# A guest place for one weight granule, the router's scores behind phase one, and a tail with other layouts and queues

## The chip, the core and the metric

The kernel runs on one core of a Trainium2 chip. TensorE (PE) multiplies matrices, VectorE (DVE) and ScalarE (ACT) work on whole tiles and copy results out of PSUM, GpSimd (POOL) and SyncE (SP) mostly issue transfers here. Transfers issued by SP, ACT and POOL are carried out by the same 16 DMA engines. The metric is the device time of one execution in microseconds (us); lower is better. Times of the trace are counted from the start of the span.

## What is computed

One layer norm of x (2048 rows of 1024) feeds two branches; their results are added to x. The first is attention over 64 segments of 32 rows with a memory of 8 rows that goes from segment to segment; the second sends the two best-scored rows through a gated feed-forward block. Cut to what matters:

```python
xn = _layernorm(x)
mem = mem0
for s in range(64):                       # 32 rows each, 32 heads of 128
    h = concatenate([mem, xn[:, 32*s:32*s + 32]], axis=1)
    q, k, v = h @ Wq, h @ Wk, h @ Wv      # by head
    p = softmax(where(mask, q @ k.T * scale, -1e9))
    o = (p @ v) @ Wo
    mem = o[:, :8]
    outs.append(o[:, 8:])
r = xn @ w_r
idx = argsort(-r)[:, :2]                  # the two routed rows
y = (silu(xn[idx] @ w_gate) * (xn[idx] @ w_up)) @ w_down
y = y * sigmoid(r[idx])
return x + concatenate(outs) + (xn + scatter(y, idx))
```

All tensors are bf16. Wq, Wk, Wv and Wo hold 8 MB each.

## The kernel before

**Granules.** The four attention weights are cut into 64 granules of 128 x 2048 (512 KB). Granules 0 to 47 belong to six phases (`PHASES`): p = 0 is the first half of Wq (granules 0 to 7), p = 1 the first half of Wk (8 to 15), p = 2 and 3 their second halves, p = 4 and 5 the halves of Wv; granules 48 to 63 are Wo. 44 are resident in SBUF; each has a home, a place of its own (`home`, `room`, `load_resident`). 17 are streamed: every segment takes them anew from a copy in DRAM (`wsc`) through five slots (`fetch`, pool `wstream`). Granule 15, the last of phase one (p = 1), is one of them. Three more (0, 7, 27) are kept partly in PSUM. The homes of Wv granules are `v_homes`: the first eight are one area, `big0`, the others stand alone; `v_homes[8]` is the home of granule 43 and `hx = v_homes[-1]` that of granule 46.

**Main rows and left rows.** Of each segment 24 rows and the 8 rows of memory are the main rows; they make the 32 columns of `ST`, and segment after segment they go through the phases (L745), attention and Wo (`project`, L798). The last 8 rows of every segment, 512 rows in all, are the left rows. Their Q and K (`left_qk`, L500) and V (`left_v`, L527) are worked out for all segments while segment 0 has the weights at hand, behind the main rows' matmuls of each phase; they go to DRAM (`ql_d`, `vl_d`), and each segment takes its own part back. What attention gives for left rows is stored after each segment in DRAM (`ol_d`, `store_sums`, L604). The tail, behind the last segment, loads all of that as `OTA` (`load_left_out`, L595, 16 loads of 256 KB: eight by POOL during the last segment, eight by SP), multiplies it by Wo (`left_rows_out`, L874, two halves of two blocks), adds x and stores four blocks (L881).

**Segment 0.** Phase zero's granules lie in homes and in four of the slots, granule 11 in the fifth. When phase p is done, `left_done(p)` fetches as many granules as slots have come free. All of the following is in program order, so each engine meets it in that order. DVE takes the row statistics of x (`row_stats`, L238) during phase zero. In phase one PE does the 32 main matmuls (L745), `left_qk` for head 0, then for heads 1 and 2; then come `spread` (four small matmuls on PE, L250, and copies on DVE, L255 to L257), which lays out means and deviations, the 16 steps of `router_tile` on DVE (a `tensor_scalar`, L263, and a multiply-and-sum, L265, on 128 x 1024 each), and `left_qk` for heads 3 to 15. `sd_rows` (L242 on DVE, a square root on ACT, L243) stands ahead of that. At the end of phase one's `left_qk` DVE copies `QKL` (L513); in the next phase ACT copies from it to `KT` (L640) and DVE copies the transposed keys there (L642), and then PE may do the scores (L650). Later the router's scores go to DRAM and come back as one row (`router_out`, `router_top`), of which DVE finds the two highest. The x tiles that statistics and router read lie in the area `big1`, over which the second half's left Q and K (`GA`) are written from phase two on.

**Feed-forward.** In the tail SP loads w_gate, w_up and w_down (`fetch_moe`, L438 and L441) into homes that have come free; `gate_up` (L903) and the down matmuls (L930) follow. POOL takes the two routed rows back out of the output (L916), DVE adds (L933), and SP stores both (L936), each behind a load of its row number into a register.

Of the kernel before, what the change touches and what calls it, by code (L numbers as in the profile page):

```python
# [21 lines left out]
HALF_KEPT = 27  # L22
KEPT_HERE = (FIRST_KEPT, NEXT_KEPT, HALF_KEPT)
NEG = -30000.0

# [4 lines left out]
def kernel(  # L30
# [86 lines left out]
    vl_d = [dram.tile([16, 16, XL, 2, P], BF16, name=f"vl_d{t}") for t in range(4)]  # L117
    ol_d = [dram.tile([16, P, XL * H], BF16, name=f"ol_d{t}") for t in range(4)]

# [88 lines left out]
    def xt(t):  # L208
        return XP[:, t // 2, (t % 2) * D:(t % 2 + 1) * D]
# [50 lines left out]

    def router_tile(t):
        XR = home(hx, [P, D], BF16, "XR")
        nc.vector.tensor_scalar(out=XR[:, :], in0=xt(t), scalar1=RI16[:, t, 0:1], scalar2=RI16[:, t, 1:2],  # L263
                                op0=ALU.subtract, op1=ALU.mult)
        nc.vector.tensor_tensor_reduce(out=XR[:, :], in0=XR[:, :], in1=WRB, scale=1.0, scalar=0.0,  # L265
                                       op0=ALU.mult, op1=ALU.add, accum_out=RF[:, t:t + 1])

# [153 lines left out]
    to_copy = list(streamed)  # L421
    flow += [(s, g) for s in range(NSEG) for g in (streamed if s else first_streamed)]

# [54 lines left out]
    for g in range(KC, 32):  # L478
        if g in first_streamed:
            if len(queued) < N_SLOT:  # L480
                fetch()
        else:
            load_resident(g)
        if g >= 8 and g < 15:
            load_x(g - 7)
    for g in v_homes[8:-1]:
        load_resident(g)
# [5 lines left out]
    def left_qk(mat, half, Gs, between, h0=0, h1=16):  # L493
        if mat == 0 and h0 == 0:
            gathered[half] = area(f"big{half}", [P, NSEG, 256], "GA")
        GA = gathered[half].rearrange("p s (m i q r) -> p s m i q r", m=2, i=4, q=4)
        for h in range(h0, h1):
            PSG = psA.tile([P, 512], F32, tag="acc", name="PSG")
            for kc in range(KC):
                nc.tensor.matmul(PSG[:, :], lhsT=part(Gs[kc], h // 4)[:, P * (h % 4):P * (h % 4 + 1)], rhs=XLT[:, :, kc, :],  # L500
                                 start=(kc == 0), stop=(kc == KC - 1))
            nc.scalar.copy(out=GA[:, :, mat, h % 4, h // 4, :], in_=PSG.rearrange("p (s r) -> p s r", r=XL))  # L502
            if h % 2 == 1 or mat + half == 0:
                next(between, None)
        if h1 < 16:
            return
        for _ in between:
            pass
        if mat == 1:
            G3 = gathered[half]  # L510
            if half == 0:
                qkl[0] = one.tile([P, 2, 2, 4, 4, XL], BF16, tag="bA", name="QKL")
            nc.vector.tensor_copy(out=qkl[0][:, half].rearrange("p m i q r -> p (m i q r)"), in_=G3[:, 0, :])  # L513
            if half == 0:
                for k in range(NSEG // 8):
                    store_left(half, k)
# [31 lines left out]
    def left_done(p):  # L548
        for g in range(8 * p, 8 * (p + 1)):
            if g in first_streamed:  # L550
                fetch()
        if p == 1:
            area("big0", [P, 8, 2048], "W8A")
# [40 lines left out]
    def load_left_out(k, queue):  # L594
        queue.dma_start(out=areas["big0"][:, 4 * k:4 * k + 4, :], in_=ol_d[k // 4][4 * (k % 4):4 * (k % 4) + 4].rearrange("s p c -> p s c"))  # L595

# [5 lines left out]
    def store_sums():  # L602
        s, t = unsaved.pop(0)
        nc.gpsimd.dma_start(out=ol_d[s // 16][s % 16], in_=t.rearrange("p r h -> p (r h)"))  # L604

# [15 lines left out]
    for s in range(NSEG):  # L621
# [7 lines left out]
        def transposes(mat, half, XB):  # L629
# [8 lines left out]
            else:  # L638
                KT[half] = one.tile([P, 16, NK], BF16, tag="kt", name="KT")
                nc.scalar.copy(out=KT[half].rearrange("p (i q) k -> p i q k", i=4)[:, :, :, 32:NK],  # L640
                               in_=qkl[0][:, half, 1, :, :, :])
                nc.vector.tensor_copy(out=KT[half][:, :, 0:32], in_=pv)  # L642

# [94 lines left out]
        for p, (mat, half) in enumerate(PHASES):  # L738
# [13 lines left out]
            if mat < 2:  # L752
# [4 lines left out]
                if s == 0:  # L757
# [4 lines left out]
                    if p == 1:  # L762
                        nc.gpsimd.tensor_copy(out=GATE, in_=gathered[0][:, 0, 128:132])
                        copy_blocks(6)
                        sd_rows(MV[:, 1:NT, :], VE[:, 1:NT])
                        left_qk(mat, half, Gs, kept, 1, 3)
                        h1 = 3
                        spread(1, NT)
                        for t in range(NT):
                            router_tile(t)  # L770
                    elif p == 2:
# [96 lines left out]
    def left_rows_out(k):  # L868
        WD = [[psK.tile([P, 512], F32, name=f"WD{2 * b + c}", tag=f"kept{2 * b + c}") for c in range(2)] for b in range(2)]
        for b in range(2):  # L870
# [7 lines left out]
            for c in range(2):  # L878
                xc = x[:, 512 * c:512 * (c + 1)]
                nc.vector.tensor_tensor(out=xc, in0=xc, in1=WD[b][c][:, :], op=ALU.add)  # L880
            nc.scalar.dma_start(out=out2.rearrange("(t s r) d -> t s r d", t=4, s=16)[2 * k + b, :, XM:SEG, :], in_=x)  # L881

# [51 lines left out]
    for c in range(2):  # L934
        v = nc.sync.value_load(I8[0:1, c:c + 1], min_val=0, max_val=S - 1)
        nc.sync.dma_start(out=routed_out(v), in_=quarters(c))  # L936

# [34 lines left out]
```

## Time and profile before

| | |
|---|---|
| median of 3 runs | 1859.54 us (1859.37 to 1860.27) |
| the profiled execution | 1847.92 us, span 1846.3 us |
| PE busy | 1555.7 us (84%) |
| DVE, ACT, POOL busy | 880.4 us, 774.9 us, 320.9 us |
| moved by DMA | 678.50 MB, mean 367 GB/s |
| segment 0 | from the start to about 242 us |
| last segment's end, tail | from about 1760 us |

All views are of the one profiled execution, which is shorter than the runs; only differences are carried over. A row of a timeline gives start and duration in us, the engine, the line of the kernel, the operation with the tiles it writes and reads, the number of merged instructions, and in brackets the idle time ahead of it with what ended that. A row of the waits gives who waited for whom, the sum in us, how often, and the longest. A row of the stretches gives start, end and length, the busy time of PE, weight loads, DVE, ACT and POOL, the granted TensorE clock (1.00 is full), the DMA engines' share and GB/s. A row that lists one line's instructions gives their least, median and greatest duration in ns and the first and last start. DMA-issuing rows of SP and ACT are marked SPq and ACTq.

### The profile page before, as it was taken

What the parts mean: (1) busy time and instruction counts of PE and PEld (TensorE: products, weight loads), DVE (VectorE), ACT (ScalarE), POOL (GpSimd) and SP (SyncE); (2) the same over time, 40 slices, a digit from 0 to 9 for tenths busy, and PEclk for the clock granted to TensorE, in tenths of its full rate; (3) what the DMA queues carried; (4) which work ended last, traced back from release to release, by engine and by line L of the source; (5) the groups of instructions that cost most, each with busy time, mean ns of one, the idle gap of its engine ahead of it and who ended that gap; (6) DMA issues with size and microseconds to landing.
All of it is one profiled execution on the core that took longest, in us unless ns stands there. A gap on an engine that the chain in (4) does not pass through costs nothing. (4 is left out here: it accounts for less than half of the span.)

```text
span 1846.3 us, 70379 instructions
## 1 busy us (share of the span) xinstructions
PE 1555.7 (84%) x30358; PEld 828.2 (45%) x30370; DVE 880.4 (48%) x2711; ACT 774.9 (42%) x2019; POOL 320.9 (17%) x592
## 2 busy tenths in 40 slices
PE   6889978888888888888888888888888888888888
PEld 3334434444444444444444444444444444444465
DVE  6631235555554454555555555444455555555420
ACT  2333134444444444444444444444444444444400
POOL 1020111111111111111111111111111111111200
PEclk9999989999999999999999999999999999999988
DMA  9684899999999999999999999999999999999996
GB/s 361 218 301 135 261 367 391 393 394 394 368 387 376 368 389 383 392 386 372 396 393 396 396 394 394 385 386 389 386 391 394 397 382 393 395 395 395 392 364 251
DMA packets 223288, 678.50 MB, mean 367 GB/s; under 512 B 46848, under 2 KB 54320, under 8 KB 222976
## 3 DMA queue, kind: packets, MB, share of 16 engines
q1 hardware_dynamic: 196768, 623.79, 88.3%
q0 software_dynamic: 24192, 46.54, 7.5%
q8 instruction: 237, 3.88, 0.8%
q10 hardware_dynamic: 2016, 3.67, 0.6%
q14 instruction: 75, 0.61, 0.1%
HBM read 652.90 MB, written 29.89 MB: 370 GB/s over the span
## 5 line engine op out<-in xcount | busy, mean ns | idle before, releaser
L745 PE MATMUL PSm<-wres,ST 128*32 128x512 bf16 x6400 | 500.7, 382 | 0.0
L745 PEld LDWEIGHTS <-ST 128*32 128x32 bf16 x12288 | 313.3, 96 | 349.5 <-issue 107.4
L745 PE MATMUL PSm<-g,ST 128*32 128x512 bf16 x3084 | 307.3, 384 | 46.6 <-DMA g<-wsc 38.2
L411 ACT COPY BK<-KEPT 128x512 bf16<-128x512 bf16 x315 | 189.3, 601 | 175.0 <-PE WO L798 65.1
L798 PEld LDWEIGHTS <-OT 128*32 128x32 bf16 x8192 | 209.2, 97 | 85.6 <-issue 69.3
L754 ACT CAST XB<-PSm 128x512 bf16<-128x512 f32 x256 | 150.2, 587 | 132.7 <-PE PSm L745 131.1
L642 DVE COPY KT<-BT 128x512 bf16<-128x512 bf16 x128 | 51.8, 405 | 290.6 <-PE BT L632 290.6
L798 PE MATMUL WO<-W8B,OT 128*32 128x256 bf16 x4096 | 186.2, 276 | 0.0
L745 PE MATMUL PSm<-W8A,ST 128*32 128x512 bf16 x2048 | 182.7, 380 | 0.0
L587 POOL DMA_DIRECT2D QKL<-ql_d x63 | 46.5, 738 | 755.7 <-ACT OTL L714 740.6
L798 PE MATMUL WO<-g,OT 128*32 128x256 bf16 x2560 | 130.7, 277 | 53.1 <-DMA g<-wsc 48.8
L832 POOL DMA_DIRECT2D out_dram<-XN x256 | 130.7, 526 | 173.9 <-DVE XN L828 173.8
L779 ACT CAST VM<-PSm 128x512 bf16<-128x512 f32 x128 | 80.3, 627 | 114.0 <-PE PSm L745 114.0
L411 DVE COPY BK<-KEPT 128x512 bf16<-128x512 bf16 x189 | 80.2, 425 | 72.3 <-ACT BK L411 36.9
L632 PEld LDWEIGHTS <-XB 128*128 128x128 bf16 x1024 | 57.9, 98 | 106.6 <-ACT XB L754 101.5
L674 DVE TENSOR_REDUCE DN<-BS 128x8 f32<-128x320 f32 x128 | 62.9, 491 | 88.0 <-ACT BS L669 88.0
L632 PE MATMUL BT<-IDENT,XB 128*128 128x128 bf16 x1024 | 101.7, 222 | 3.1
L500 PE MATMUL PSG<-XLT,wres 128*128 128x512 bf16 x352 | 101.3, 390 | 0.8 <-ACT GA L502 0.7
L637 ACT COPY QT<-BT 128x512 bf16<-128x512 bf16 x128 | 74.9, 585 | 53.4 <-PE BT L632 51.4
L659 DVE TENSOR_TENSOR BS<-BS,CT 128x96 f32<-128x96 f32 (+1 forms) x256 | 59.7, 233 | 76.5 <-PE BS L652 72.0
L745 PE MATMUL PSm<-BK,ST 128*32 128x512 bf16 x567 | 76.7, 388 | 22.2 <-DVE ST L369 22.2
L828 DVE CAST XN<-WO 128x256 bf16<-128x256 f32 x64 | 27.2, 424 | 127.5 <-PE WO L798 127.5
(171 smaller groups left out, 2278.9 us busy)
## 6 DMA issues: line engine op xcount, KB each, us to landing
g<-wsc SPq DMA_DIRECT2D x1071, 512.0 KB, 6.3
ql_d<-GA POOLq DMA_DIRECT2D x16, 512.0 KB, 6.3
QKL<-ql_d POOLq DMA_DIRECT2D x63, 128.0 KB, 6.2
MW<-in_B_w_gate_dram SPq DMA_DIRECT2D x16, 448.0 KB, 8.0
MW<-in_B_w_down_dram SPq DMA_DIRECT2D x14, 512.0 KB, 8.3
wres<-in_A_Wk_dram SPq DMA_DIRECT2D x12, 512.0 KB, 10.5
MW<-in_B_w_up_dram SPq DMA_DIRECT2D x12, 448.0 KB, 8.5
XP<-in_A_x_dram SPq DMA_DIRECT2D x8, 512.0 KB, 10.1
```

Of the source, the lines that this page charges most:

```text
L411: copy(out=back[g][c], in_=KEPT_COLS[g][c])
L500: nc.tensor.matmul(PSG[:, :], lhsT=part(Gs[kc], h // 4)[:, P * (h % 4):P * (h % 4 + 1)], rhs=XLT[:, :, kc, :], start=(kc == 0), stop=(kc = ...
L632: nc.tensor.transpose(out=PTq[:, il, :, :].rearrange("p j r -> p (j r)"), in_=XB[:, il * P:(il + 1) * P], identity=IDENT[:, :])
L637: nc.scalar.copy(out=QT[half][:, :, :], in_=pv)
L642: nc.vector.tensor_copy(out=KT[half][:, :, 0:32], in_=pv)
L659: nc.vector.tensor_tensor(out=S4, in0=S4, in1=m, op=ALU.add)
L674: nc.vector.tensor_reduce(out=DN[:, :], in_=S8, axis=AX.X, op=ALU.add)
L745: nc.tensor.matmul(PSm[32 * jq:32 * jq + 32, :], lhsT=ST[:, kc, :], rhs=part(Gv, jq), start=(kc == 0), stop=(kc == KC - 1), tile_position= ...
L754: nc.scalar.copy(out=XB[:, :], in_=PSm[:, :])
L779: nc.scalar.copy(out=VM[half][:, :], in_=PSm[:, :])
L798: nc.tensor.matmul(PS[32 * g:32 * g + 32, 0:256], lhsT=lhs(h), rhs=Gv[:, D * hs + 256 * g:D * hs + 256 * (g + 1)], start=False, stop=(last ...
L832: nc.gpsimd.dma_start(out=out2[s * SEG:s * SEG + XM, 256 * g:256 * (g + 1)], in_=OB[32 * g:32 * g + XM, :])
```

## The change

Granule 15 is no longer fetched through a slot in segment 0. It is loaded, early and in its turn behind granule 14, into the home of granule 43 (`v_homes[8]`), as a guest; granule 43 is loaded there when phase one is done, ahead of the `big0` loads on SP. The fetches of segment 0 after that come one place earlier.

`sd_rows`, `spread` and the router's 16 steps move from the middle of phase one to the end of phase zero (`left_done(0)`); the steps now alternate between two buffers. The copy of `QKL` (both halves) and segment 0's copies of transposed keys go from DVE to ACT.

In the tail `ol_d` is laid out by partition, so that a load takes 2 KB in one piece for each partition where it took four pieces of 512 bytes; a store writes its 128 pieces of 512 bytes at a distance of 8 KB. The four stores of left rows go from ACT to POOL. The two routed rows are stored by SP and ACT, one each, with row numbers loaded ahead of the activation.

```diff
-    ol_d = [dram.tile([16, P, XL * H], BF16, name=f"ol_d{t}") for t in range(4)]
+    ol_d = [dram.tile([P, 16, XL * H], BF16, name=f"ol_d{t}") for t in range(4)]
...
-    def router_tile(t):
-        XR = home(hx, [P, D], BF16, "XR")
...
+    def router_tiles():
+        XR = home(hx, [P, 2, D], BF16, "XR")
+        for t in range(NT):
+            nc.vector.tensor_scalar(
+                out=XR[:, t % 2, :], in0=xt(t), scalar1=RI16[:, t, 0:1], scalar2=RI16[:, t, 1:2],
+                op0=ALU.subtract, op1=ALU.mult)
+            nc.vector.tensor_tensor_reduce(out=XR[:, t % 2, :], in0=XR[:, t % 2, :], in1=WRB, scale=1.0, scalar=0.0,
+                                           op0=ALU.mult, op1=ALU.add, accum_out=RF[:, t:t + 1])
...
-    flow += [(s, g) for s in range(NSEG) for g in (streamed if s else first_streamed)]
+    flow += [(s, g) for s in range(NSEG) for g in (streamed if s else first_streamed) if s or g != GUEST]
...
     for g in range(KC, 32):
-        if g in first_streamed:
+        if g == GUEST:
+            t = res_tiles[g] = room(v_homes[8], "guest")
+            nc.sync.dma_start(out=t, in_=granule_dram(g))
+        elif g in first_streamed:
...
-    for g in v_homes[8:-1]:
+    for g in v_homes[9:-1]:
         load_resident(g)
...
-            nc.vector.tensor_copy(out=qkl[0][:, half].rearrange("p m i q r -> p (m i q r)"), in_=G3[:, 0, :])
+            nc.scalar.copy(out=qkl[0][:, half].rearrange("p m i q r -> p (m i q r)"), in_=G3[:, 0, :])
...
     def left_done(p):
         for g in range(8 * p, 8 * (p + 1)):
-            if g in first_streamed:
+            if g in first_streamed and g != GUEST:
                 fetch()
-        if p == 1:
+        if p == 0:
+            sd_rows(MV[:, 1:NT, :], VE[:, 1:NT])
+            spread(1, NT)
+            router_tiles()
+        elif p == 1:
+            res_tiles.pop(GUEST)
+            load_resident(v_homes[8])
             area("big0", [P, 8, 2048], "W8A")
...
-        queue.dma_start(out=areas["big0"][:, 4 * k:4 * k + 4, :], in_=ol_d[k // 4][4 * (k % 4):4 * (k % 4) + 4].rearrange("s p c -> p s c"))
+        queue.dma_start(out=areas["big0"][:, 4 * k:4 * k + 4, :], in_=ol_d[k // 4][:, 4 * (k % 4):4 * (k % 4) + 4, :])
...
-        nc.gpsimd.dma_start(out=ol_d[s // 16][s % 16], in_=t.rearrange("p r h -> p (r h)"))
+        nc.gpsimd.dma_start(out=ol_d[s // 16][:, s % 16, :], in_=t.rearrange("p r h -> p (r h)"))
...
-                nc.vector.tensor_copy(out=KT[half][:, :, 0:32], in_=pv)
+                (nc.vector.tensor_copy if s else nc.scalar.copy)(out=KT[half][:, :, 0:32], in_=pv)
...
                     if p == 1:
                         nc.gpsimd.tensor_copy(out=GATE, in_=gathered[0][:, 0, 128:132])
                         copy_blocks(6)
-                        sd_rows(MV[:, 1:NT, :], VE[:, 1:NT])
-                        left_qk(mat, half, Gs, kept, 1, 3)
-                        h1 = 3
-                        spread(1, NT)
-                        for t in range(NT):
-                            router_tile(t)
...
-            nc.scalar.dma_start(out=out2.rearrange("(t s r) d -> t s r d", t=4, s=16)[2 * k + b, :, XM:SEG, :], in_=x)
+            nc.gpsimd.dma_start(out=out2.rearrange("(t s r) d -> t s r d", t=4, s=16)[2 * k + b, :, XM:SEG, :], in_=x)
...
+    ends = (nc.sync, nc.scalar)
...
+    end_rows = [ends[c].value_load(I8[0:1, c:c + 1], min_val=0, max_val=S - 1) for c in range(2)]
     SG = T2[:, 64:64 + 4 * FC].bitcast(F32)
...
     for c in range(2):
-        v = nc.sync.value_load(I8[0:1, c:c + 1], min_val=0, max_val=S - 1)
-        nc.sync.dma_start(out=routed_out(v), in_=quarters(c))
+        ends[c].dma_start(out=routed_out(end_rows[c]), in_=quarters(c))
```

More of the change, by code (lines that the diff above doesn't have):

```diff
@@ L23 @@
 KEPT_HERE = (FIRST_KEPT, NEXT_KEPT, HALF_KEPT)
+GUEST = 15
 NEG = -30000.0
@@ L259 @@
     hx = v_homes[-1]
-    def router_tile(t):
-        XR = home(hx, [P, D], BF16, "XR")
[L263 to L266, printed above, removed]
+    def router_tiles():
[6 more added lines that the diff above has]
+                                           op0=ALU.mult, op1=ALU.add, accum_out=RF[:, t:t + 1])
     def router_out():
```

## The prediction, made before the changed kernel was run

> **What bounds the kernel now.** I read the page first, then PE's waits in two stretches, then timelines around the long waits. The page's slices:
>
> ```profile
> span 1846.3 us, 70379 instructions
> ...
> PE   6889978888888888888888888888888888888888
> ...
> PEclk9999989999999999999999999999999999999988
> DMA  9684899999999999999999999999999999999996
> ```
>
> A slice is 46 us. From the sixth on DMA is full and PE is not; the first five, which hold segment 0, are the only place inside the kernel where DMA has room. PE's waits from 250 us to 1740 us, then those up to 250 us:
>
> ```profile
> PE WO L798 <- DMA g<-wsc: 44.8, 86, 1.8
> PE PSm L745 <- DMA g<-wsc: 38.2, 88, 1.5
> ```
>
> ```profile
> PE BS L650 <- ACT KT L640: 6.7, 1, 6.7
> PE PSm L745 <- DMA g<-in_A_Wk_dram: 5.5, 1, 5.5
> PE WO L798 <- DMA g<-in_A_Wo_dram: 3.1, 2, 2.8
> PE PSV L527 <- ACT VM L779: 2.2, 1, 2.2
> ```
>
> In the middle PE waits for streamed granules, and the stream restarts each transfer when PE frees a slot. So segments 1 to 63 are a chain that takes its length from bytes moved and its start from the end of segment 0. The change leaves the chain alone and acts before and behind it. In segment 0 two single waits stand out, 6.7 and 5.5 us; the change is aimed at both.
>
> **The guest.** Granule 15 is asked for only when phase zero frees a slot, at 51.98, and PE stands before it:
>
> ```profile
> 29.34 0.38 SPq L205 DMA_DIRECT2D XP<-in_A_x_dram  x1
> 30.62 7.19 SPq L136 DMA_DIRECT2D wres<-in_A_Wq_dram  x6
> ...
> 51.98 0.33 SPq L386 DMA_DIRECT2D g<-in_A_Wk_dram  x1
> ```
>
> ```profile
> 53.06 0.83 PE L745 MATMUL PSm<-wres,ST 128*32 128x512 bf16 x12
> ...
> 60.73 0.62 PE L745 MATMUL PSm<-g,ST 128*32 128x512 bf16 x4 [5.54 <-DMA g<-in_A_Wk_dram]
> ```
>
> ```profile
> 60.70:64.70 4.00, 3.97 (x13) 1.32 (x13) 0.00 (x0) 0.58 (x1) 0.00 (x0) 0.50 0.48 189
> ```
>
> ```profile
> wres<-in_A_Wk_dram SPq DMA_DIRECT2D x12, 512.0 KB, 10.5
> ```
>
> The last x tile is issued at 29.34, so the guest goes out between it and 30.62 and lands some 10.5 us later, near 41, twelve before its use. Term A: -5.5. After the wait the granted clock is 0.50 for 4.0 us of dense matmuls, which take twice their time: term B, -2.0 (0 to -2.3). Bytes do not change: granule 43 is loaded later by as much as the guest is early, so what SP issues between (phases two and three) is one transfer later, about 1.3 us by SP's pace there (7.19 for six), with 30 us of cover. Granule 43's load stands on SP behind one fetch and ahead of the eight `big0` loads, which then are about 1.3 us later; both are for phases four and five, and this stretch shows the room:
>
> ```profile
> 126.00:175.00 49.00, 45.15 (x307) 20.47 (x307) 14.61 (x35) 21.18 (x35) 4.38 (x7) 1.00 0.37 120
> ```
>
> **The router.** DVE before:
>
> ```profile
> 53.44 0.18 DVE L242 TENSOR_SCALAR MISC<-MISC 128x15 bf16<-128x15 bf16 x1
> 68.78 0.87 DVE L255 COPY BS<-BT 96x30 f32<-96x30 f32 x4 [15.16 <-PE BT L250]
> ...
> 69.80 0.45 DVE L263 TENSOR_SCALAR XR<-XP,MISC 128x1024 bf16<-128x1024 bf16 x1
> ...
> 99.27 0.22 DVE L513 COPY QKL<-GA 128x256 bf16<-128x256 bf16 x1
> ```
>
> ```profile
> 53.16 0.59 ACT L502 CAST GA<-PSG 128x512 bf16<-128x512 f32 x1 [1.36 <-PE PSG L500]
> ...
> 91.16 0.58 ACT L502 CAST GA<-PSG 128x512 bf16<-128x512 f32 x1 [1.14 <-PE PSG L500]
> 99.58 0.30 ACT L640 COPY KT<-QKL 128x128 bf16<-128x128 bf16 x1 [7.83 <-DVE QKL L513]
> ```
>
> ```profile
> 91.06 1.05 PE L745 MATMUL PSm<-wres,ST 128*32 128x512 bf16 x16
> ...
> 92.81 0.39 PE L745 MATMUL PSm<-wres,ST 128*32 128x512 bf16 x4
> 99.93 0.23 PE L650 MATMUL BS<-KT,QT 128*32 128x40 bf16 x4 [6.73 <-ACT KT L640]
> ```
>
> ```profile
> 99.90:103.00 3.10, 3.07 (x42) 1.24 (x43) 1.89 (x6) 0.58 (x1) 1.17 (x3) 0.53 1.02 407
> ```
>
> The router holds DVE from 69.80 to 99.27, 29.5 us or 1.84 a tile; `QKL` is queued behind it, `KT` behind that, PE behind `KT`. DVE had lain idle for 15.16 us before. Now `spread` comes at the end of phase zero, and PE meets it at 53.06: statistics end at 53.62, the square root follows ACT's eviction of 53.75 and takes about 0.2 (an estimate, from the 0.18 of DVE's step on the same 15 columns), so the four small matmuls run near 54.0 to 54.2. Queued behind them on PE is all of phase one. Term C, the added wait: +1.0 (0.6 to 1.5).
>
> Phase one then ends 5.5 + 2.0 - 1.0 = 6.5 earlier, at 84.5 for 91.0. The router starts as long after `spread`'s first copy as before (69.80 - 68.78 = 1.0), so near 55.4 for a copy near 54.4, and ends at 84.9. Nothing in phase one needs DVE. Two buffers change little, since both steps run on the one engine; I cost them at nothing (0 to -1.6 for sixteen times 0.1, off the path). PE reaches the scores at 86.7. On ACT the last eviction ends at 85.2, then the `QKL` copy (0.4, between 0.30 for 128 columns and 0.59 for 512), `KT` from it (0.3) behind PE's transposes, and the transposed keys (0.6), now on ACT too: 86.9 with the hand-over. A wait of about 0.3 stays of 6.7: term D, -6.4 (-5.9 to -6.7). The low clock after it (0.53 for 3.1 us) goes as well: term E, -1.5 (0 to -1.6).
>
> Half one pays for ACT's extra copies without any gain, as DVE was free there: scores about 0.4 later, and the chain over DVE, exponent and L779 on which PE waits 2.2 is later by that. Term F: +0.4 (0 to +0.6).
>
> POOL's first six granule copies are issued behind head 0's eviction, so about 7 us earlier and beside the router, and must write while early loads end. Before, POOL issued eight stores beside it:
>
> ```profile
> 92.04 4.47 POOL L519 DMA_DIRECT2D ql_d<-GA  x8 [22.86 <-ACT GA L502]
> ```
>
> That is 0.56 each, no different from its 0.57 elsewhere (below), and the copies are first read in segment 1: nothing. Everything later in segment 0 (W8B, Wo, the stream) is issued behind PE's progress, so it moves along. Segment 0: -5.5 - 2.0 + 1.0 - 6.4 - 1.5 + 0.4 = -14.0.
>
> The Trainium skill (TensorE: Matmul & The Clock Gate, Part 1) says that an idle window of about 3.4 us halves the clock and a busy one restores it. The trace agrees after both waits (0.50, 0.53); by it the new wait of 1 us costs no clock, and if it did, C would be about +3.
>
> **The tail.** Loads of left sums, and rates without and with them:
>
> ```profile
> L595 POOL DMA_DIRECT2D OTA<-ol_d x8: 747/749/781, 1746.8 to 1752.0; - x8
> ```
>
> ```profile
> 1755.75 0.62 PE L798 MATMUL WO<-g,OT 128*32 128x256 bf16 x8 [2.19 <-DMA g<-wsc]
> ...
> 1759.21 0.62 PE L798 MATMUL WO<-g,OT 128*32 128x256 bf16 x8 [1.13 <-DMA g<-wsc]
> ```
>
> ```profile
> 1780.00:1787.00 7.00, 6.95 (x33) 4.63 (x33) 0.00 (x0) 0.00 (x0) 0.00 (x0) 1.00 1.03 408
> 1790.00:1795.00 5.00, 5.00 (x194) 4.97 (x193) 1.28 (x2) 0.00 (x0) 0.00 (x0) 0.74 1.17 317
> ```
>
> Full DMA moves 408 GB/s with weights alone and 317 while SP's left sums go along. Eight loads are 2.1 MB: 6.6 us at 317, 5.1 at 408. Those that POOL issues run beside the last two granules PE waits for, 2.19 and 1.13. At most 1.5 us come free there, but the loads may also take a larger share of each turn. I take half, term G: -0.7 (-1.6 to +1.0). SP's eight gain as much, but PE is then at gate and up and later waits for no load: nothing.
>
> The four stores go to POOL. Only the last matters, since POOL fetches the routed rows behind it and DVE adds into them:
>
> ```profile
> 1835.79 1.21 POOL L916 DMA_DIRECT2D T<-out_dram  x2 [73.17 <-DMA out_dram<-XLS]
> ```
>
> ```profile
> T<-out_dram POOLq DMA_DIRECT2D x2, 2.0 KB, 2.5
> ```
>
> ```profile
> 1840.74 0.48 DVE L933 SCALAR_TENSOR_TENSOR T<-YP,SIG,T 128x256 bf16<-128x256 f32 x1 [5.91 <-PE YP L930]
> ```
>
> ```profile
> L604 POOL DMA_DIRECT2D ol_d<-OTL x64: 556/573/580, 247.9 to 1753.8; - x64
> ```
>
> The two fetches are issued by 1837.0; DVE starts at 1840.74, released by PE. At 2.5 us from issue to landing about 1.2 us are free. A store from POOL costs 0.57 to issue: nothing, +1 if it lands 2 us later. SP's two final stores:
>
> ```profile
> L936 SPq DMA_DIRECT2D out_dram<-T x2: 602/650/698, 1841.2 to 1843.3; - x2
> ```
>
> The second starts 2.1 us behind the first, with a register load between; on ACT it starts with the first. Term H: -2.0 (-1.5 to -2.1). Nothing hides it, as the span ends on that store.
>
> The strided stores of `ol_d` are the unknown in the chain: no row shows 512-byte pieces written 8 KB apart. 64 KB a segment are 0.16 us at 408 and 0.21 at 317 GB/s: +0.05 x 64 = +3.2 at the upper end, nothing at the lower, since pieces were 512 bytes before. I take nothing.
>
> **Sum.** -14.0 - 0.7 - 2.0 = -16.7. The profiled execution, 1847.92, would become 1831.2. It lies 11.6 below the median, far outside the spread of the runs (0.9), so the profile slightly changes the pace; I carry the difference over: 1859.54 - 16.7 = 1842.8.
>
> **Rivals.** *The gain is taken back at the end of segment 0.* PE waits there 3.1 us for Wo granules through slots. If DMA were the bound from the start, these waits would grow by most of the 14. For it: DMA is full from there on. Against: DMA share is 0.37 from 126 to 175, and those transfers are issued only when PE frees room. Half taken back: 1859.5 - 7 - 2.7 = 1850.
>
> *The strided stores slow the chain* (the other side). They decide from 16.7 / 64 = 0.26 us a segment, over the 0.21 that such a store takes at all at the worse rate. At double that rate's time for the store and its neighbours held up as long again, 0.4 a segment, it is +26 - 16.7: 1869. Against: they move 64 KB in a segment of about 24 us.
>
> *DVE stays the bound.* The x tiles lie under the second half's `GA`, whose first eviction falls near 88.5 now (two microseconds past the scores). The router ends at 84.9; from 2.07 us a tile on, PE would wait again, at 0.2 us a tile more by 3. It ran at 1.84 beside the same evictions. At 2.4 a tile: +5, so 1848.
>
> *The left sums' loads cost no more in small pieces.* Then 317 GB/s has another cause, such as the store beside it, G is 0 and the time 1843.5. The Trainium skill (DMA: Bandwidth & Descriptors, Specifications) speaks for this: it gives 512 bytes as the least transfer for line rate. The trace disagrees so far as those two stretches go, 317 against 408.
>
> **How the numbers follow.** The forecast (1842.8, its own range 1838 to 1847 by the bounds of C to H) has 0.66, small pieces at no cost 0.10, taken back 0.10, DVE still the bound 0.04, slower by the stores 0.07, the change showing no effect (guest and moved router not on the path after all) 0.03. The range from 1838 to 1851 leaves out the slower case and some of the rest. Within 0.2% (3.7 us), about what a measurement can tell from no change, lies 0.03; faster 0.90; slower 0.07.
>
> **What would show it.** Right: PE's wait for `g<-in_A_Wk` gone, a wait near 1 us at L250, the one at L650 under 1 us, the router between 55 and 85, granted clock 1.00 from 60 to 105, segment 1 starting near 228 for 242; the last two stores starting together. Wrong: longer waits of L798 before 235, a longer segment in the middle, evictions of phase two behind the router, POOL's fetch of routed rows ending later than PE's last matmul.

## The result and the profile after

The changed kernel takes 1840.17 us (median of 5 runs, 1829.70 to 1844.92) against 1859.37 for the kernel before (median of 5 runs in the same comparison): a ratio of 0.990, 95% interval 0.987 to 0.993. Two later comparisons gave 0.990 (0.987 to 0.993) and 0.990 (0.986 to 0.994). The forecast was 1842.8 in a range of 1838 to 1851. The profiled execution took 1829.70, with a span of 1828.1 for 1846.3 before.

The page of the changed kernel, the same slices as before:

```profile
span 1828.1 us, 70401 instructions
...
PE   6999888888888888888888888888888888888888
...
PEclk9999899999999999999999999999999999999988
DMA  9785999999999999999999999999999999999996
```

PE's second and third slices rise from 8 to 9: they hold phase one and the start of phase two. From the seventh on all three rows are as before. PE's waits up to 250 us, changed kernel:

```profile
...
PE WO L804 <- DMA g<-in_A_Wo_dram: 4.0, 2, 3.7
PE PSV L533 <- ACT VM L785: 2.2, 1, 2.2
...
PE BT L251 <- ACT MISC L244: 0.8, 1, 0.8
```

The waits of 6.7 us for `KT` and 5.5 us for `g<-in_A_Wk_dram` are gone from the list, and the new one at `spread`, 0.8, is there. One stretch shows what became of them, from the first matmuls of phase one to the scores. First the kernel before, then the changed one (columns as in the prediction: start, end and length, busy time of PE, weight loads, DVE, ACT and POOL, clock, DMA share, GB/s):

```profile
53.00:100.00 47.00, 34.73 (x210) 14.95 (x213) 30.39 (x59) 11.54 (x21) 8.76 (x17) 0.88 0.63 217
```

```profile
53.00:85.50 32.50, 32.28 (x204) 14.35 (x203) 28.02 (x54) 11.72 (x21) 4.69 (x10) 1.00 0.68 235
```

The stretch is 14.5 shorter. PE stood still in it for 47.00 - 34.73 = 12.3 us and now for 0.2: the waits. Its busy time fell by 2.4, of which 0.2 is `spread`, whose four matmuls lie just ahead of the second stretch; the clock rose from 0.88 to 1.00, so the rest is the half clock behind the first wait.

Since single terms are smaller than the scatter of the runs, every profiled execution is cut here in three: from the start to the first cast of segment 0's output (`XN<-WO` on DVE), from there to the same cast 62 segments later, and the rest with segment 63 and the tail. The column "phase one" gives when PE is done with phase zero and comes to phase one.

| kernel | median us, ratio (95%) | phase one | segment 0 ends | 62 segments | rest |
|---|---|---|---|---|---|
| before | 1859.37 | 53.1 | 241.0 | 1490.7 | 114.6 |
| changed | 1840.17, 0.990 (0.987 to 0.993) | 52.1 | 225.5 | 1489.9 | 112.7 |
| changed, again | 1839.49, 0.990 (0.987 to 0.993) | 52.8 | 226.8 | 1500.7 | 118.7 |
| changed, third | 1837.76, 0.990 (0.986 to 0.994) | 52.5 | 227.3 | 1494.4 | 114.7 |
| guest alone | 1848.26, 0.996 (0.994 to 0.999) | 53.7 | 236.2 | 1502.1 | 113.1 |
| router alone | 1846.88, 0.993 (0.991 to 0.996) | 53.8 | 234.7 | 1490.6 | 115.4 |
| guest and router | 1843.90, 0.993 (0.990 to 0.996) | 51.6 | 226.9 | 1488.7 | 114.6 |
| tail alone | 1855.68, 0.999 (0.996 to 1.002) | 51.0 | 243.1 | 1511.1 | 114.3 |
| both ends on SP | 1838.96, one run | 53.3 | 226.8 | 1497.7 | 112.7 |
| copies on DVE | 1843.50, one run | 51.9 | 226.7 | 1500.6 | 114.5 |
| router step twice | 1854.99, one run | 52.3 | 242.1 | 1496.8 | 114.5 |
| one routed row | 1836.62, one run | 51.7 | 225.3 | 1495.2 | 114.5 |
| everything small | 1840.41, 0.992 (0.989 to 0.995) | 54.1 | 229.1 | 1496.7 | 110.3 |
| table early | 1835.05, 0.988 (0.984 to 0.993) | 53.9 | 227.8 | 1493.3 | 110.9 |

Each ratio is to runs of the kernel before beside it, with medians of 1859.37 for the first pair of rows, 1858.70 for the four kernels that split the change, 1857.57 for *changed, again* and *everything small*, 1856.00 for *changed, third* and *table early*; the one-run kernels stand beside one of before of 1859.39. The first column of numbers is of runs, the others of one profiled execution each. Segment 0 is 13.7 to 15.5 shorter in the changed kernel. Phase one is reached at 51.0 and 53.1 by the two kernels with the front of before and at 51.6 to 53.9 by those with the whole front as changed: up to 2.9 us of a difference between two rows can lie ahead of all that the change touches. The rest shows no change beyond its scatter, and the middle differs by 22 us between executions, which the last section looks at.

### The profile page after: what moved, and what is told of

It is laid out like the page before. It is cut to its first block, busy times and chain, and to the rows that moved or that the text cites. A ratio compares the mean times of both kernels' runs of the same rounds, so it can differ in the third digit from the quotient of the medians.

```text
span 1828.1 us, 70401 instructions
## 1 busy us (share of the span) xinstructions
PE 1552.2 (85%) x30370; PEld 827.1 (45%) x30370; DVE 878.1 (48%) x2707; ACT 776.9 (42%) x2023; POOL 321.0 (18%) x596
## 5 line engine op out<-in xcount | busy, mean ns | idle before, releaser
L785 ACT CAST VM<-PSm 128x512 bf16<-128x512 f32 x128 | 80.1, 625 | 114.3 <-PE PSm L757 114.3
L686 DVE TENSOR_REDUCE DN<-BS 128x8 f32<-128x320 f32 x128 | 62.9, 492 | 85.4 <-ACT BS L681 85.4
## 6 DMA issues: line engine op xcount, KB each, us to landing
MW<-in_B_w_down_dram SPq DMA_DIRECT2D x14, 512.0 KB, 10.9
```

What stands on the lines that cost most here:

```text
L686: nc.vector.tensor_reduce(out=DN[:, :], in_=S8, axis=AX.X, op=ALU.add)
L785: nc.scalar.copy(out=VM[half][:, :], in_=PSm[:, :])
```

## The experiments

**The front's two halves apart, and the tail alone.** Four kernels split the change. *Guest alone* keeps `spread` and the router in phase one:

```diff
-        if g in first_streamed:
+        if g == GUEST:
+            t = res_tiles[g] = room(v_homes[8], "guest")
+            nc.sync.dma_start(out=t, in_=granule_dram(g))
+        elif g in first_streamed:
...
+            res_tiles.pop(GUEST)
+            load_resident(v_homes[8])
```

> The kernel before with the guest granule alone. Theory (each of the two waits is a loss of its own and the chain of segments carries a gain unchanged): PE's 5.5 us before granule 15 and the 2.0 us of half clock go, so segment 0's last cast (240.99 before) ends about 7.5 us earlier, near 233.5; the router still stands in the middle of phase one, starts 7.5 us earlier too, and PE's wait at the scores (6.7) stays, 6 to 7 us. Time about 7.5 us below before. Rival (the router alone sets the end of segment 0's early part, PE waits at the scores whatever comes before): the wait at the scores grows to 14 us and segment 0 ends as before. Second rival (the gain is taken back by transfers at the end of segment 0): PE's waits for Wo there grow from 5 to 12 us.

Two waits and a stretch of that kernel:

```profile
PE BS L656 <- ACT KT L646: 6.7, 1, 6.7
PE WO L804 <- DMA g<-in_A_Wo_dram: 4.0, 2, 2.9
```

```profile
60.70:64.70 4.00, 4.00 (x24) 1.86 (x22) 2.95 (x10) 1.17 (x2) 1.54 (x4) 1.00 1.02 410
92.70:97.00 4.30, 4.27 (x45) 1.65 (x46) 1.79 (x6) 0.58 (x1) 1.72 (x4) 0.50 1.03 402
```

No wait for granule 15 is left, and where the clock was 0.50 before it is full. The wait at the scores stands untouched at 6.7, followed by a half clock that lasts at least 4.3 us; so these two causes are apart. The scores come 7.2 earlier, at 92.73 (terms A and B together: 7.5), and 7.9 earlier if counted from phase one, which PE reached 0.7 later. But segment 0 ends only 4.8 earlier, for the 7.5 expected. From the first half's scores to the second's it takes 0.9 longer, under the half clock, and between the first output matmul and the cast 1.2 longer, with 0.9 of it in the wait for Wo granules, 4.0 for 3.1. This may be the rival "taken back at the end of segment 0", at a small size; *tail alone*, which has the front of before, is 0.6 longer there too.

*Router alone* leaves granule 15 in its slot:

```diff
+        if p == 0:
+            sd_rows(MV[:, 1:NT, :], VE[:, 1:NT])
+            spread(1, NT)
+            router_tiles()
...
-                        spread(1, NT)
-                        for t in range(NT):
-                            router_tile(t)
```

> The kernel before with the router behind phase zero and the copies on ACT, without the guest. Theory: the wait at the scores falls from 6.7 us to under 1, the half clock after it goes (1.5), half one pays up to 0.4; the wait of about 1 us for the spread is hidden, since PE then waits less for granule 15, which still lands near 60.7 (4.5 us for 5.5). Segment 0 ends near 233.5 (7.5 us earlier). Rival (the spread's wait comes on top and the router beside the evictions is slowed): less than 6 us gained, router over 1.9 us a tile.

Its wait and the row at the scores:

```profile
PE PSm L751 <- DMA g<-in_A_Wk_dram: 4.1, 1, 4.1
```

```profile
94.00 0.21 PE L656 MATMUL BS<-KT,QT 128*32 128x40 bf16 x4 [0.17 <-ACT KT L648]
```

The wait at the scores falls from 6.73 to 0.17 with the guest left out, and segment 0 ends 6.3 earlier, for the 7.5 expected. The wait for the granule, 5.5 before, is 4.1 here behind 0.8 at `spread`: PE waits a little sooner for something else and no longer in all.

*Guest and router* is all of the front, with the tail as before:

> Guest, router and copies on ACT, with the tail of before. Theory (segment 0 is nearly all of the gain): segment 0 ends 14 to 15.5 us earlier as in the changed kernel, and the time is within 2 us plus noise of the changed kernel, 14 to 18 us below before. Rival (the tail's edits or the strided stores give or take several us in the chain): the time differs from the changed kernel by 5 us or more.

Segment 0 ends at 226.9, 14.1 earlier: the front's gain is the changed kernel's. It is 3.0 more than 4.8 and 6.3 together, but 2.1 of that is phase one, reached at 51.6 here and at 53.7 by the guest alone; that the two halves help each other is not shown.

*Tail alone*:

```diff
-    ol_d = [dram.tile([16, P, XL * H], BF16, name=f"ol_d{t}") for t in range(4)]
+    ol_d = [dram.tile([P, 16, XL * H], BF16, name=f"ol_d{t}") for t in range(4)]
...
-            nc.scalar.dma_start(
+            nc.gpsimd.dma_start(
...
-        v = nc.sync.value_load(I8[0:1, c:c + 1], min_val=0, max_val=S - 1)
-        nc.sync.dma_start(out=routed_out(v), in_=quarters(c))
+        ends[c].dma_start(out=routed_out(end_rows[c]), in_=quarters(c))
```

> The kernel before with the tail's edits alone (layout of the left sums, stores on POOL, final stores on SP and ACT). By the prediction's terms: PE's waits for the last two granules fall by 0.7, the last store starts 2 us earlier, 2.7 us in all. By the trace of the changed kernel (ACT's final store waits until SP's has landed; waits for the last granules 4.9 for 4.0): the last store starts no more than 0.3 us earlier relative to DVE's last add, the whole within 1 us of before apart from the chain's own spread. If strided stores cost something, segments 1 to 63 take longer by 0.05 us each or 3 us in all.

0.999 (0.996 to 1.002): nothing that can be measured. Its rest is 114.3 for 114.6. It also gives a second look at the front of before: PE comes to phase one at 51.0 and waits 7.9 for granule 15, where it was 5.5. The matmul that waits for it starts at 61.04 here, at 60.73 before and at 61.07 with the router alone, whenever PE got there. So term A is worth more the sooner PE is done with phase zero.

**What holds the last store.** The changed kernel's rows for the final line, and for the tile that is stored, the time from issue to landing (of four transfers, the two fetches of routed rows and the two stores):

```profile
L943 ACTq EVENT_SEMAPHORE  x5: 38/38/5841, 1815.0 to 1825.1; - x5
...
L943 SPq DMA_DIRECT2D out_dram<-T x1: 692/692/692, 1823.3 to 1823.3; - x1
...
L943 ACTq DMA_DIRECT2D out_dram<-T x1: 1143/1143/1143, 1825.2 to 1825.2; - x1
```

```profile
DMA to landing us min/median/max: 1.8/2.7/3.5
```

ACT has its row number at hand. Its longest semaphore wait, 5.8 us, is for POOL's fetch of the routed rows and is over at 1820.9, well before DVE's last add; a later one ends at 1824.98, released by SP's store, which was issued at 1823.26 and so had landed 1.7 later. Then ACT issues. The two stores do not start together; they are 1.9 apart where they were 2.0. *Both ends on SP* takes the other queue away and keeps the early row numbers:

```diff
-    ends = (nc.sync, nc.scalar)
+    ends = (nc.sync, nc.sync)
```

> The changed kernel with both final stores on SP, row numbers loaded early as there. From DVE's last add to the span's end it took 5.5 us before and 5.3 in the changed kernel. Theory (the second store is held until the first has landed, because both write the output at a row not known beforehand): the second store starts 1.7 to 2.0 us behind the first though no register load stands between, and the end comes 5.2 to 5.5 us after the add. Rival (the prediction's: the register load between the stores made the 2.1 us): the second starts 0.7 us behind the first and the end comes 1.3 us sooner, about 4.1 us after the add.

```profile
L943 SPq DMA_DIRECT2D out_dram<-T x2: 561/629/697, 1832.7 to 1834.5; - x2
```

1.7 apart (1832.75 and 1834.48) on one queue too, although no issue takes over 0.7: neither the register load nor the queue makes the gap, and it equals the landing of a store. The end comes 5.0 behind the add, a little sooner than the 5.2 to 5.5 expected. In the kernel before, the register load lay over that wait: it ran from 1841.99 to 1843.02, and the first store had landed near 1842.96 (an estimate, 1841.25 + 1.71 as in the other kernels). *One routed row* leaves out the store of the second routed row, so that row of the output stays without its feed-forward:

```diff
-    for c in range(2):
+    for c in range(1):
         ends[c].dma_start(out=routed_out(end_rows[c]), in_=quarters(c))
```

> The changed kernel without the second of the two final stores (one routed row is not stored, so the output lacks its feed-forward part). It shows what a second store that costs nothing would give: by the theory that the second waits for the first's landing (1.7 us) and then takes its own time, the end comes about 3.3 to 3.6 us after DVE's last add for 5.3, 1.7 to 2.0 us less. Rival (the end is set by something else behind the stores): 5 us or more as now.

From the start of DVE's last add to the end of the span it takes 4.3, against 5.5 before, 5.3 changed and 5.0 with both on SP: more than the 3.3 to 3.6 expected. The landing of the last store tells more than the end of the span. It comes 4.2 after the start of that add before, 4.2 in the changed kernel, 3.9 with both on SP, and 2.2 with one store. So the change gained nothing at the landing, and its 0.2 lie in what the span still holds behind it. With one store the span ends 2.1 behind the landing, for 1.1 in the changed kernel, and the row that fills this time is POOL's last long instruction of the program:

```profile
L974 POOLq DRAIN  x3: 46/115/7970, 1826.2 to 1834.7; - x3
```

It begins with POOL's second fetch of a routed row, lasts 8.0 us here and in the changed kernel, and ends at 1834.16, 3.5 after the add's start at 1830.67; the closing steps of all engines follow at once. In the changed kernel it ends before the last store has landed. What it waits for is not shown. So the end has two bounds, and a second store that cost nothing would gain 1.2 against the kernel before, not 2.0, because the other bound is met. The two later kernels that also have both stores on SP end 5.8 and 6.0 behind the add for the same reason: their last store has landed at 3.9 too, and the drain ends at 5.0 and 5.2.

The Trainium skill (DMA: Bandwidth & Descriptors, Issuing engines are not separate DMA queues) says that several issuing engines save only the time of issuing. These runs agree: with two queues the last store lands 0.3 later than with one, as ACT takes 1.14 to issue it and SP 0.56.

**Whether the copies had to leave DVE.** *Copies on DVE* undoes only that:

```diff
-            nc.scalar.copy(out=qkl[0][:, half]...
+            nc.vector.tensor_copy(out=qkl[0][:, half]...
...
-                (nc.vector.tensor_copy if s else nc.scalar.copy)(out=KT[half][:, :, 0:32], in_=pv)
+                nc.vector.tensor_copy(out=KT[half][:, :, 0:32], in_=pv)
```

> The changed kernel with the copies of QKL and of segment 0's transposed keys back on DVE, as before the change. Theory (the router's new place alone removes the wait at the scores, since it ends about 1.5 us before phase one's last eviction): PE's wait at the scores of half zero stays under 0.5 us, both halves' scores come 0.1 to 0.4 us earlier, segment 0 ends within 0.5 us of the changed kernel (213.6 us after PE's first transpose). Rival (the copies had to leave DVE for the wait to go): the wait at the scores is 2 us or more.

DVE and PE of that kernel:

```profile
83.72 0.23 DVE L519 COPY QKL<-GA 128x256 bf16<-128x256 bf16 x1 [2.01 <-ACT GA L508]
84.41 0.43 DVE L654 COPY KT<-BT 128x512 bf16<-128x512 bf16 x1 [0.46 <-PE BT L644]
```

```profile
84.96 0.19 PE L662 MATMUL BS<-KT,QT 128*32 128x40 bf16 x4
```

DVE lies idle for 2.0 ahead of the copy, as the router is done, and PE reaches the scores without any wait. Term D comes from the router's place alone; the copies on ACT added nothing. Counted from phase one, the first half's scores come 0.3 sooner than in the changed kernel and the second half's no sooner.

**How much room the router has.** *Router step twice* does each tile's multiply-and-sum a second time, into an unused place:

```diff
+            nc.vector.tensor_tensor_reduce(out=XR[:, t % 2, :], in0=XR[:, t % 2, :], in1=WRB, scale=1.0, scalar=0.0,
+                                           op0=ALU.mult, op1=ALU.add, accum_out=TWICE[:, t:t + 1])
```

> The changed kernel with each router step's multiply-and-sum done twice (the second into numbers that nothing reads). A step takes 1.73 us there, so 3.0 now, and sixteen end near 54.3 + 47.5 = 101.7 for 81.9. Theory (DVE becomes the bound again once the router ends later than the first eviction into the second half's left Q, which lies over the x tiles, near 88.0): ACT's first eviction of phase two is held to about 102, PE waits some 12 to 14 us there, segment 0 ends that much later. Rival (nothing in phase two hangs on the router as the copies are on ACT, DVE only has to be done by the router's output): no wait longer than 2 us, segment 0 ends within 2 us of the changed kernel.

ACT, PE and a stretch of that kernel:

```profile
100.00 1.07 ACT L511 CAST GA<-PSG 128x512 bf16<-128x512 f32 x2 [13.05 <-DVE XR L266]
```

```profile
PE PSG L509 <- ACT GA L511: 10.8, 1, 10.8
```

```profile
100.00:106.00 6.00, 5.36 (x13) 1.93 (x13) 4.12 (x10) 1.66 (x3) 0.19 (x1) 0.50 0.99 266
```

At 2.99 us a tile the rival "DVE stays the bound" is real. ACT's first eviction of phase two waits for the last read of an x tile until 100.00, where it was at 87.98 in the changed kernel; PE stands 10.8 us (12 to 14 were expected), and the clock is 0.50 for the 6 us behind. Segment 0 ends 16.6 later, at 242.1. From the first half's scores to the second's it takes 77.4 for 63.6, which is the 10.8 and some 3 for the 6 us at half clock; 2.6 more come behind that, in a stretch that differs by up to 1.9 between kernels with the whole front as changed, and stay unexplained. By the prediction's rule PE's wait would be (2.99 - 2.07) x 16 = 14.7; the room was larger than the rule has it (below). The Trainium skill (TensorE: Matmul & The Clock Gate, Part 1) has the clock halved after an idle window of about 3.4 us; this wait of 10.8 halved it, and the wait of 0.8 at `spread` did not.

**A better version.** *Everything small* put the copies back on DVE, moved `spread` a few matmuls into phase one, put both ends on SP, and loaded ACT's table for the Silu and cleared `YP` ahead of the last gate and up matmuls:

> The changed kernel with five small edits: spread and router issued behind phase one's third granule, copies back on DVE, both final stores on SP, a dummy activation that loads the Silu table ahead of time, and the down sums' memset ahead of the gate matmuls. Theory (each takes its wait off the path): spread's 0.8 us to 0.1, copies 0.4, end 0.3, the 2.2 us between gate and down matmuls to about 0.7; segment 0 near 212.5 and the stretch behind the last gate matmul 1.5 us shorter, 2.5 to 3 us below the changed kernel, little beside the spread of the runs. Rival (TensorE's clock windows eat it, or the router now ends too late): segment 0 not shorter, the stretch between gate and down over 2 us.

Beside it ran the changed kernel again:

> The changed kernel again, for its time beside the kernel before on one chip and for a second trace of it. Theory (segment 0 carries nearly all of the change, the chain's length differs from run to run for reasons outside the change): segment 0's last cast again 213 to 214.5 us after PE's first transpose, time 13 to 19 us below before. Rival (part of the gain seen first was a short chain by chance): less than 10 us below.

The edits gained nothing over it: 1840.41 against 1839.49. The trace splits that. The rest is the shortest of all, 110.3, but segment 0 ends at 229.1, later than in any execution of the changed kernel. Of the 3.6 against the first of these, 2.0 are phase one, reached at 54.1, ahead of all the edits; from there to the scores it takes 0.3 less, and behind the scores 1.8 more. Inside phase one `spread` still stops PE, now for DVE's copies:

```profile
PE BT L640 <- DVE BS L256: 0.7, 1, 0.7
```

By this trace the front edits are worth 0.3. So the last study kept the front as changed, and took the table, the clearing and SP's ends:

```diff
+    nc.scalar.activation(out=T2[:, 0:2], in_=T2[:, 100:102], func=ACTF.Silu)
+    YP = psA.tile([P, 512], F32, tag="acc", name="YP")
+    nc.vector.memset(YP[:, 0:256], 0.0)
     gate_up(early, len(pieces))
```

> The changed kernel, with the table for the Silu loaded ahead of the last gate and up matmuls, YP cleared there too, and both last stores on SP. If the wait of 2.2 us before the down matmuls is the table and the clearing (the changed kernel's trace: ACT loads the table for 1.28 us behind the last gate and up matmul), it falls to about 0.6 as in the kernel with everything small, and what lies behind segment 63 shortens by 1.6 plus 0.3 for the two stores: about 1.9 us, 0.1% of the time, less than these rounds can tell, so the trace has to show it: last start of L928's successor to end. If instead the shorter stretch of the kernel with everything small came from the clock's phase, the stretch from the first gate and up matmul to the first down matmul stays at 44 to 45 us.

> The changed kernel as it is, beside the one above. Near 0.990 of the kernel before; segment 0 ending between 225.3 and 226.9 us; the length of the 62 segments behind it is open, as it was 1489.9 and 1500.7 in two executions of this kernel. If that length goes with the DMA rate, 389 GB/s from 260 to 1700 us comes with about 1490 and 386 with about 1500 again.

Segment 0 ended a little outside what was expected of the two repeated executions of the changed kernel: 214.7 us after PE's first transpose for at most 214.5, and at 227.3 for at most 226.9. Their ratios came out as expected. PE's wait ahead of the down matmuls, first in the changed kernel, then with the table early:

```profile
PE YP L938 <- DVE YP L932: 2.2, 1, 2.2
```

```profile
PE YP L939 <- DVE T L933: 0.6, 1, 0.6
```

That wait is 1.6 shorter, as worked out (the table and the clearing were moved together, so their shares are not shown). The end behind DVE's add takes 0.4 more, as POOL's drain of 8.0 us now holds it, and the rest is 110.9 for 112.7 to 118.7 of the three executions of the changed kernel. Its 1835.05 is the lowest median of all, but 0.988 (0.984 to 0.993) against 0.990 (0.986 to 0.994) does not separate the two: that it beats the changed kernel is shown by the trace for this one wait and not by the times.

## Why the prediction was right, point by point

**Segment 0, forecast at -14.0**: -15.5 in the compared profile, -13.2 to -15.7 in all kernels that have the whole front as changed. The mechanism is the one worked out. 1.0 of the -15.5 lies ahead of phase one; counted from there, these kernels show -12.6 to -14.5.

- *A and B* (-5.5, -2.0): SP issues the guest behind the last x tile, and PE uses it without a wait, with the clock full:

```profile
30.75 0.33 SPq L484 DMA_DIRECT2D guest<-in_A_Wk_dram  x1
```

```profile
52.87 0.25 PE L251 MATMUL BT<-MISC 128*128 128x30 bf16 x4 [0.80 <-ACT MISC L244]
53.05 0.83 PE L757 MATMUL PSm<-wres,ST 128*32 128x512 bf16 x12
...
55.12 0.39 PE L757 MATMUL PSm<-guest,ST 128*32 128x512 bf16 x4
```

The prediction has the fetch of granule 15 wait for a slot that phase zero frees. That is not all of it: in *tail alone* SP issues it at 52.32, 1.35 after PE has left phase zero, behind its own earlier loads and the landing of one of them. The guest goes out ahead of those, so it takes away both causes. The size of A was one execution's: 5.5 and 7.9 stand in the two traces that have the front of before.
- *C* (+1.0): 0.8, the 0.80 in the first of these rows, and it costs no clock.
- *D* (-6.4): the wait at the scores is 0.17, so -6.56. The wait that stays is for ACT's copies, as forecast; that ACT had to do them is not borne out. DVE's router, then ACT and PE up to the scores:

```profile
54.25 0.45 DVE L265 TENSOR_SCALAR XR<-XP,MISC 128x1024 bf16<-128x1024 bf16 x1
...
80.08 0.54 DVE L265 TENSOR_SCALAR XR<-XP,MISC 128x1024 bf16<-128x1024 bf16 x1
...
81.81 0.08 DVE L268 DVE_READ_ACCUMULATOR2_ANT MISC<- 128x1 f32 x1
```

```profile
83.90 0.41 ACT L519 COPY QKL<-GA 128x256 bf16<-128x256 bf16 x1
...
87.98 0.58 ACT L508 CAST GA<-PSG 128x512 bf16<-128x512 f32 x1 [1.25 <-PE PSG L506]
```

```profile
85.48 0.21 PE L662 MATMUL BS<-KT,QT 128*32 128x40 bf16 x4 [0.17 <-ACT KT L654]
```

- *The router* was forecast from 55.4 to 84.9 and ran from 54.25 to 81.9, 27.6 us or 1.73 a tile. Two buffers, costed at nothing with a bound of sixteen times 0.1, did save 0.12 a tile, 1.9 in all and a little over the bound of 1.6, off the path. The room was mis-sized the safe way: the last x tile was read by 80.6 (L265 at 80.08) and the eviction that has to wait for it came at 87.98, so PE would be held from about 1.73 + 7.4 / 16 = 2.2 us a tile on, where the prediction said 2.07.
- *E* (-1.5): from the first half's scores to the second's it took 65.0 before and 63.6 after, -1.4. *F* (+0.4): from the second half's scores to the first Wo matmul 62.8 and 62.9, so +0.1; PE's wait for `VM` is 2.2 as before. Other kernels with the whole front show +0.3 to +2.1 there, so the size of F is not settled.
- *Taken back* (rival): the wait for Wo granules grew from 3.1 to 4.0, but the stretch from the first Wo matmul to the cast by only 0.2. Other kernels with the whole front show 0.0 to +0.8 there. Of 14 us little was lost; the guest alone lost 1.2 there.

**The tail, forecast at -2.7**: this is the part that failed: H outside its bounds, G inside them but not gained. *H* (-2.0, bounds -1.5 to -2.1) is the wrong step: "on ACT it starts with the first". The last store lands as late as before, since the second store is let go only when the first has landed, 1.7 after its issue, and the register load had lain over that wait; the span's end comes 0.2 sooner, and 1.2 would be the most to have. *G* (-0.7, bounds -1.6 to +1.0): PE's waits for the last granules, in the list from 1735 us on before and from 1722 us on after:

```profile
PE WO L798 <- DMA g<-wsc: 4.0, 3, 2.2
```

```profile
PE WO L804 <- DMA g<-wsc: 4.9, 2, 2.7
```

Segment 63 took 28.4 for 28.2. In segment 63 of all executions these waits come to 3.7 to 4.4 with the layout of before and 3.8 to 5.2 with the new one. So G is nothing, or slightly against. The eight loads of SP did get their rate back. Changed kernel, from 1766 to 1775, while they go along:

```profile
1766.00:1775.00 9.00, 9.00 (x116) 6.61 (x115) 1.28 (x2) 0.00 (x0) 0.51 (x1) 1.00 1.03 403
```

403 GB/s for the 317 of the prediction's row, which shows the worst 5 us; over all eight, from the first issue to the last landing, it is 402 for 347. In the changed kernel a piece is 2 KB, so the rival "left sums' loads cost no more in small pieces" was wrong on the rate and right on the time, as PE waits for none of it. The Trainium skill (DMA: Bandwidth & Descriptors, Specifications) gives 512 bytes as enough for line rate; the two rates speak against that here.

**The strided stores, costed at nothing, up to +3.2.** They did not bring the rival's +26: the changed kernel's 62 segments took 1489.9 in the compared profile, against 1490.7. Whether they cost a few us is not settled. Over all profiled executions the middle is 1497.6 on average with them (ten) and 1493.0 without (four), with single values that differ by 22; the times, on the other side, give the changed kernel 0.990 and the front alone 0.993.

**The sum.** Segment 0 of the three executions of the changed kernel is 13.7 to 15.5 shorter, and the rest -1.9, +4.1 and +0.1. The stages so come to some -14. The medians say -19.2 with an interval of 12 to 25, and -18 in two later comparisons; no stage of these traces shows the 4 or 5 us between, and the middle scatters by far more. The forecast of -16.7 is right in its size because the front, which holds 14 of it, was right. The tail's 2.7 were a miss of over 2 us that the measurement of the total can't see, and that the total came out beyond the forecast and not short of it is luck of the runs.

The prediction also took the profiled execution before, 11.6 below its median, for a sign that the profile changes the pace. Later runs of the kernel before range from 1842.57 to 1868.57, so 1847.92 lies within the scatter of runs. That execution of the changed kernel is the shortest of its five runs in the same way.

## What to carry to other kernels

Work that one engine does in the middle of a phase may sit ahead of a small copy that everything else waits for; move the long work to where the engine is idle, and count its room by the next write over what it still reads. A wait of several us costs more than its length, since the clock behind it is low; take the wait away and the clock comes with it. A store to an address known only at run time may be held for the store before it, whatever queue it stands on: look at what the second one waits for before counting on two queues, and at what else the end of the program waits for.

## What was not expected of the hardware

The middle of the kernel, 62 segments of the same work, took 1488.7 to 1511.1 us in the profiled executions. The stretch from 260 to 1700 us of the changed kernel, of its second execution, and of the tail alone:

```profile
260.00:1700.00 1440.00, 1213.56 (x26876) 648.45 (x26870) 731.69 (x2340) 669.85 (x1801) 264.77 (x480) 1.00 1.02 389
```

```profile
260.00:1700.00 1440.00, 1209.42 (x26717) 642.12 (x26716) 729.34 (x2333) 665.79 (x1790) 262.66 (x475) 1.00 1.01 386
```

```profile
260.00:1700.00 1440.00, 1206.75 (x26502) 642.02 (x26494) 722.82 (x2313) 662.05 (x1780) 261.03 (x472) 0.99 1.01 384
```

389 GB/s goes with 1489.9, 386 with 1500.7, 384 with 1511.1, and the third execution of the changed kernel had 388 and 1494.4. This says little more than the lengths do: the 62 segments move 578 to 579 MB in every execution, so a longer middle has a lower rate whatever made it longer. The DMA engines are full in all of them. The clock is part of it at most: the two longest, *tail alone* and *guest alone*, have 37.5 us at half clock in this stretch, the others 10 to 27, but the first two executions of the changed kernel have 13.7 each and differ by 10.9. Which comes first, slower transfers that let PE stand until the clock falls, or a clock that falls and lets slots come free later, no run here tells apart; it stays open. What it means for reading is plain: terms below 3 us in a kernel of 1850 are told by a stage of the trace that lies outside this stretch, and not by the time of a run.
